# The second layer's output matrix by seven products of blocks per pair instead of eight, with the four pairs written as one order of steps

## Chip, cores and metric

The kernel runs on one core of a Trainium2 chip. The metric is the device time in microseconds (us) of one execution, median of several. TensorE (PE in the rows) does the matrix products, with PEld its weight loads; VectorE (DVE), ScalarE (ACT) and GpSimd (POOL) do elementwise work; SyncE (SP) issues nearly all transfers, which then run on 16 DMA engines.

## The reference

```python
p_packed = sm_attn(p, k, v)                    # 8 x 8 heads, 576 tokens, 32 packed, head size 64
x = heads_joined(sm_attn(q, p_packed, p_packed))            # 4608 x 512
h = x @ w_in                                                # first layer, 512 x 2048
x = (h * sigmoid(1.702 * h)) @ w_out                        # 2048 x 512
g = x @ w_gate                                              # second layer, 512 x 1536
out = (g * sigmoid(g) * (x @ w_val)) @ w_out2               # 1536 x 512, out is 4608 x 512
```

All of it is fp32. The kernel keeps that precision by splitting each operand into a rounded high part and the rest, and by three passes per product (high by high, high by rest, rest by high; `mm3`). A product of 128 x 128 weights with 512 columns is thus three matmuls.

## The kernel before

**The first layer** runs over 8 batches of 576 tokens, two halves each, 16 steps per half. Next to it the next batch's attention and, late, the second layer's weights are made ready: `prep` splits sums and differences of blocks of w_gate and w_val and stores them to `w2s` in DRAM, `split_wo2` splits w_out2 (12 tiles of 128 x 512, kept in SBUF).

**The second layer** takes the 4608 tokens in nine blocks of 512. Block 0 goes alone (`single`, 12 units). The others go in four pairs. For each of 12 column groups m of 128, `quad` computes gate and value of both blocks by seven block products in place of eight; one product is 6 matmuls (`prod`). VectorE and ScalarE add them up in `c1`, `c2`, `c3`, apply tanh, and leave the gated result g of one block in `gh` (split at once by ACT and POOL) and that of the other in the tile `g{m}`. Between the products stands the output matrix of an earlier group: `fill` calls `p5`, which for each of four groups of 128 tokens takes `gh` as weights and w_out2's tile m as 512 columns: 12 matmuls per block and group, into four PSUM banks `acc`. After the 12th group `halve` copies the banks to SBUF, and rows of 512 floats (2 KB) go to `out`, 16 stores of 32 rows per block.

The gv products rotate over four PSUM banks (`ps_h`, `ps_a`, two each). Weights of the next groups come from `w2s` by `load_w` into ten buffers of pool `z_p`. In this part the order on each engine is that in which the tile framework schedules the code; in the first part of the kernel it is a text (`FIRST`) that `issue` reads, with `pin["on"]` set so that each engine keeps that order.

Of the kernel before, what the change touches and what calls it, by code (L numbers as in the profile page):

```python
# [111 lines left out]


@with_exitstack
def kernel(
# [102 lines left out]
    w2s = dram.tile([NM2, 4, P, 2, 512], F32, name="w2s")  # L218

# [529 lines left out]

    def open_m2():  # L750
        p = pools2["m"] = tc.alloc_tile_pool(name="m2", bufs=1, reuse_waits="tile")
# [4 lines left out]
        k2["gh"] = [wo_p.tile([P, 2, TB], F32R, tag="wo1", name="gh") for _ in range(4)]  # L756

# [138 lines left out]
    def gh_of(key):  # L896
        if key not in gt:
            gt[key] = k2["gh"][k2.setdefault("ngh", 0) % 4]
            k2["ngh"] += 1
        return gt[key]  # L900

    def p5(n, m, ts, outs):
        y = gt[n, m]
        if m == 0 and 0 in ts:
            for t in range(4):
                acc[t] = ps_acc.tile([P, 512], F32, tag=f"acc{t}", name="acc")
        for t in ts:
            mm3(acc[t], lambda a: y[:, a, t * P:(t + 1) * P], lambda c: wo2[m][:, c], m == 0, m == NM2 - 1)
            if m == NM2 - 1:
                o = k2[outs[t]]  # L910
                halve(o, acc[t], t % 2)
                b0 = (n * TB + t * P) // 32
                for k0 in range(4):
                    b, j = divmod(b0 + k0, NBLK)
                    eng = ACT if n == NB2 - 1 and k0 % 2 else SP
                    eng.dma_start(out=out[b * S:(b + 1) * S].rearrange("(i n) e -> n i e", n=NBLK)[j],
                                  in_=o[32 * k0:32 * k0 + 32])
        if 3 in ts:
            gt.pop((n, m))

    def split_g2(n, m):
        if n and n % 2 == 0:
            split(gh_of((n, m)), k2["g", m], DVE)

    OUT1, OUT2 = ("c1", "c2", "c3", "s2"), tuple(("g", m) for m in range(4, 8))
    units2 = [(p, m) for p in range(-1, NPAIR) for m in range(NM2)]
    groups = [(n, m) for n in range(NB2) for m in range(NM2)]

    def fill(k, ts=(0, 1, 2, 3)):
        if k >= 0:  # L930
            n, m = groups[k]
            if 0 in ts and k + 2 < len(groups):
                split_g2(*groups[k + 2])
            p5(n, m, ts, OUT1 if n % 2 else OUT2)

    def quad(i, k):

        p, m = units2[i]
        c1, c2, c3, s1, s2, ta, tb = (k2[x] for x in ("c1", "c2", "c3", "s1", "s2", "ta", "tb"))

        def p7(j, a, b):
            q, t = ((ps_h, "h"), (ps_a, "a"))[(i + j) % 2]
            ps = q.tile([P, 512], F32, tag=t, name="gv")
            prod(ps, i, a, b, True)
            return ps

# [24 lines left out]

    def single(m, k):
# [10 lines left out]
        split(gh_of((0, m)), s1, POOL)  # L983
# [32 lines left out]
    for n in range(NU, len(units)):  # L1016
# [35 lines left out]
    for i, (p, m) in enumerate(units2):  # L1052

        k = i - 2 + NM2 * max(p, 0) if p or m > 1 else -1
        last = m == NM2 - 1
        if p < 0:
            single(m, k)
            for part in range(4):
                if m:
                    prep(m + 1, part)  # L1060
            if last:
                load_w(i + 1)
                fill(k + 1)
            for _ in range(2):
                if steps and (len(steps) > 4 or last):
                    steps.pop(0)()
# [53 lines left out]
```

## Time and profile before

| | |
|---|---|
| median of 3 runs | 1642.13 us (1642.01 to 1644.1) |
| profiled execution | 1641.24 us, its span 1639.5 us |
| PE busy | 1618.8 us, 99% of the span |
| PEld / DVE / ACT / POOL busy | 1446.4 / 1138.6 / 764.8 / 279.1 us |
| granted TensorE clock | 0.999 on the mean |
| second layer | from 816 us on: block 0 to 915 us, the pairs to the end |

The span runs from the first to the last instruction; 1.74 us of the execution lie around it. Busy time of an engine is a sum over stages; what a stage costs is read in that stage's own stretch.

### The profile page before, as it was taken

How to read it: one execution, taken by the hardware profiler on the slowest of the kernel's cores; microseconds unless marked ns; L12 is line 12 of the kernel's file. 1: busy time of each engine (PE TensorE's matmuls, PEld its weight loads, DVE VectorE, ACT ScalarE, POOL GpSimd, SP SyncE). 2: the span in 40 equal slices, each digit the busy share in tenths (PEclk: the TensorE clock that was granted, in tenths of full speed). 3: DMA queues.
4: the chain of work that ended last, by engine and by line, in shares of the span. 5: the costliest groups of instructions: out<-in, count | busy, mean ns of one | idle time of the engine just before them, and what ended most of it. 6: DMA issues, size and time to landing. Idle time of an engine off the chain costs nothing.

```text
span 1639.5 us, 25914 instructions
## 1 busy us (share of the span) xinstructions
PE 1618.8 (99%) x9346; PEld 1446.4 (88%) x9346; DVE 1138.6 (69%) x2152; ACT 764.8 (47%) x1629; POOL 279.1 (17%) x235
## 2 busy tenths in 40 slices
PE   8999999999999999999999999999999999999998
PEld 7799999999999999999988888888888888888887
DVE  7988786876869777685894566756566656846562
ACT  5876667565656757564652222332233222422222
POOL 1342131231313123020221110000100001000010
PEclk9999999999999999999999999999999999999999
DMA  9987757475655737253887444435443544425411
GB/s 316 315 268 225 208 170 241 156 223 149 214 186 167 243 114 241 73 194 104 288 315 279 155 154 159 149 109 163 156 158 110 174 139 155 143 79 185 141 46 52
DMA packets 169345, 291.66 MB, mean 178 GB/s; under 512 B 58624, under 2 KB 96000, under 8 KB 169216
## 3 DMA queue, kind: packets, MB, share of 16 engines
q1 hardware_dynamic: 168832, 289.47, 54.1%
q8 instruction: 74, 1.21, 0.3%
q10 hardware_dynamic: 384, 0.52, 0.1%
q14 instruction: 55, 0.45, 0.1%
HBM read 227.02 MB, written 62.91 MB: 177 GB/s over the span
## 4 chain that ended last, share of the span: by engine, by line
PE 83%; DVE 8%; issue 4%; ACT 2%; DMA 2%; POOL 0%; SPq 0%; DVEq 0%; ACTq 0%
PE acc L151 35%; PE gv L151 30%; PE h L151 10%; PE sc L151 3%; PE zp L151 2%; PE pv L151 2%; DVE z L151 1%; DVE gh L151 1%; DVE g L151 1%; DVE x L151 1%; PE idle L151 1%; DMA wh<-win 1%; ACT z L151 1%; PE a1T L151 0%; DVE c L151 0%
## 5 line engine op out<-in xcount | busy, mean ns | idle before, releaser
L151 PE MATMUL gv<-xh,w 128*128 128x512 f32 x2304 | 554.4, 389 | 0.0
L151 PEld LDWEIGHTS gv<-xh,w 128*128 128x128 f32 x2304 | 432.5, 188 | 89.7
L151 PE MATMUL acc<-gh,wo 128*128 128x288 f32 x3072 | 454.0, 296 | 0.8 <-DVE gh L151 0.6
L151 PEld LDWEIGHTS acc<-gh,wo 128*128 128x128 f32 x3072 | 424.3, 188 | 5.7 <-DVE gh L151 1.4
L151 PE MATMUL acc<-wo,gh 128*128 128x512 f32 x1296 | 326.9, 389 | 0.4
L151 PEld LDWEIGHTS acc<-wo,gh 128*128 128x128 f32 x1296 | 243.0, 188 | 52.0 <-DVE c L151 1.7
L151 PE MATMUL h<-a,z 128*128 128x288 f32 x1536 | 251.3, 298 | 1.0 <-DVE g L151 0.9
L151 DVE TENSOR_TENSOR gh<-g,gh 128x288 fp32r<-128x288 f32 (+1 forms) x285 | 170.5, 598 | 89.4 <-ACT gh L151 86.7
L151 PEld LDWEIGHTS h<-a,z 128*128 128x128 f32 x1536 | 220.5, 188 | 9.9 <-DVE g L151 3.0
L151 ACT CAST gh<-g 128x288 fp32r<-128x288 f32 (+1 forms) x304 | 140.4, 462 | 157.1 <-DVE g L151 104.4
L151 POOL TENSOR_TENSOR gh<-s,gh 128x512 fp32r<-128x512 f32 x60 | 82.3, 1372 | 699.1 <-ACT gh L151 655.4
L151 DVE TENSOR_TENSOR c<-gv,c 128x512 f32<-128x512 f32 x192 | 132.3, 689 | 84.0 <-ACT tb L151 56.6
L151 ACT CAST gh<-s 128x512 fp32r<-128x512 f32 x60 | 37.3, 621 | 248.0 <-DVE s L151 248.0
L151 DVE SCALAR_TENSOR_TENSOR g<-sig,h 128x288 f32<-128x288 f32 x256 | 114.1, 446 | 42.8 <-ACT sig L151 39.8
L151 ACT ACTIVATE sig<-h 128x288 f32<-128x288 f32 x256 | 104.5, 409 | 78.2 <-PE h L151 75.9
L151 DVE TENSOR_TENSOR ta<-gv,c 128x512 f32<-128x512 f32 x96 | 66.1, 689 | 83.3 <-PE gv L151 83.3
L151 POOL TENSOR_TENSOR z<-z,z 128x512 fp32r<-128x512 f32 x51 | 69.7, 1367 | 151.6 <-ACT z L151 151.6
L151 DVE TENSOR_TENSOR z<-zp,z 64x512 f32<-64x512 f32 (+1 forms) x120 | 81.9, 682 | 14.9 <-ACT z L151 12.2
L151 ACT ACTIVATE s<-c 128x512 f32<-128x512 f32 x48 | 30.4, 632 | 96.5 <-DVE c L151 96.5
L151 PE MATMUL zp<-wh,E 128*128 128x512 f32 x224 | 66.9, 400 | 5.0 <-DVE z L151 2.5
L151 ACT COPY z<-zp 64x512 f32<-64x512 f32 x112 | 65.1, 581 | 12.4 <-PE zp L151 9.7
L151 ACT ACTIVATE s<-ta 128x512 f32<-128x512 f32 x48 | 30.3, 632 | 69.0 <-DVE ta L151 69.0
(133 smaller groups left out, 1504.0 us busy)
## 6 DMA issues: line engine op xcount, KB each, us to landing
w<-w2s SPq DMA_DIRECT2D x144, 512.0 KB, 3.2
wh<-win SPq DMA_DIRECT2D x96, 512.0 KB, 4.0
w2s<-w SPq DMA_DIRECT2D x36, 512.0 KB, 3.7
w<-w2s SPq DMA_DIRECT2D x48, 256.0 KB, 2.7
vt<-in_v_dram SPq DMA_DIRECT2D x80, 128.0 KB, 3.4
x2d<-x SPq DMA_DIRECT2D x16, 576.0 KB, 3.2
w2d<-f SPq DMA_DIRECT2D x36, 256.0 KB, 3.1
w64in<-in_moe_w_in_dram SPq DMA_DIRECT2D x16, 512.0 KB, 8.7
```

Source lines behind the costliest of these rows:

```text
L151: x = getattr(self.engine, name)(*a, **k)
```

## The change

**Seven products for the output matrix.** For a pair of blocks, g (1024 tokens by 1536) and w_out2 (1536 by 512) are seen as 2 x 2 blocks each. Seven products of block sums replace eight products of blocks. Each has 6 chunks of 128 along the inner dimension (numbered k) and two halves e of 128 output columns; one `pt n e` is three matmuls of 512 columns. There are 42 chunks n per pair, listed in `SUMS`: n 0 to 11 belong to products 0 and 1 in turn, then six each to products 2 to 6. Weights and columns change sides: a 128 x 128 piece of the weight sums is now loaded as weights and the 512 tokens of g are the columns, so that the result comes out transposed.

**Weight sums.** `sums` computes the four sums of blocks of w_out2 during the last batch of the first layer (steps 6 to 17), splits them on ACT and POOL and stores them to a new DRAM tensor `w5s`; `split_wo2` stores its own tiles there too (18 stores of 256 KB). `load_wo2` starts at step 18 instead of 5. In the pairs, `lw5` loads two chunks (512 KB) at a time into four buffers.

**Sums of g.** `ts` (four per k, DVE) turns the gated results, now in `g1` and `g`, into block sums in place; `hi n` (ACT) and `lo n` (POOL or DVE) split chunk n into one of five `gh` buffers. `fd` and `f4` add the banks' contents into the output blocks, `tr` transposes 32 x 32 squares on DVE, and `od j e a` stores 32 output columns of 512 tokens: pieces of 32 floats (128 bytes), in two transfers where the 512 tokens cross a batch.

**One written order.** The text `SECOND` lists 2452 steps for the four pairs (675, 625, 625, 527; a plus sign marks a step of the next pair), read by `issue` with `pin` on. Besides those above: `pr j x` is product x of unit j (6 matmuls), `c1`, `t1`, `tb`, `t2` are the unit's ACT steps, `e1` to `e6`, `b5`, `u1`, `u2`, `g1`, `g2` its DVE steps, `xa`, `xh`, `xl` prepare the next pair's tokens, `lw` and `lx` load gate weights and tokens.

```diff
+    TURN = [NK * (j % 2) + j // 2 for j in range(NM2)]
+    SUMS = [(j % 2, j // 2) for j in range(NM2)] + [(j, k) for j in range(2, 7) for k in range(NK)]
...
         split(wo2[m], x32.pop(("o", m)), POOL if m % 2 else DVE)
         load_wo2(m + 5)
+        h, k = divmod(m, NK)
+        SP.dma_start(out=w5_of(h, k), in_=wo2[m][:, :, :256].bitcast(F32))
+        if h:
+            SP.dma_start(out=w5_of(5, k), in_=wo2[m][:, :, 256:].bitcast(F32))
...
+        def pt(n, e):
+            j, k = SUMS[n]
+            b = 2 * (j % 2) + e
+            if k == 0:
+                ab[b] = ps_acc.tile([P, 512], F32, tag=f"acc{b}", name="acc")
+            w, y = w5[p, n // 2][:, n % 2], oper[p, n]
+            mm3(ab[b], lambda a: w[:, a, e * P:(e + 1) * P], lambda c: y[:, c], k == 0, k == NK - 1)
...
+        def fd(j, e):
+            ps, v, u = ab[2 * (j % 2) + e], (c1, c2)[e], (c3, s2)[e]
+            if j == 0:
+                ACT.activation(v, ps, AF.Copy, scale=0.5)
...
+                    eng = ACT if p == NPAIR - 1 and j == 6 and a % 2 else SP
+                    eng.dma_start(out=out[b * S:(b + 1) * S].rearrange("(i n) e -> i n e", n=NBLK)[:, k:k + c, e0:e0 + 32],
+                                  in_=y[:, t:t + c])
...
             if u == 5:
+                load_sums(0)
+            if 6 <= u < 18:
+                sums(*divmod(u - 6, 2))
+            if u == 18:
                 for i in range(5):
                     load_wo2(i)
```

Two pieces of the text for the second pair, the end of its last unit and the passage to the next pair:

```
pr 11 6; hi 11; xa 0 0; lw5 8; hi 14; b5 11; lx 5; xh 0 4; lo 14 dve; lo 11 pool; pt 10 0; +lw 2 1; xh 0 6; e6 11;
pt 10 1; fd 0 0; e5 11; pt 11 0; t2 11; xa 0 1; hi 15; pt 11 1; u2 11; xh 0 2; pt 12 0; lw5 9; lo 15 pool; fd 0 1;
hi 16; pt 12 1; g2 11; pt 13 0; ts 5 1; pt 13 1; lo 16 dve; hi 17; pt 14 0; lw5 10; fd 1 0; hi 18; lo 17 pool
```

**Where instructions now stand.** On TensorE, in the middle of a pair, one unit before (gv are the gate and value products, acc the output matrix, w and wo their tiles):

```order
L151 MATMUL gv<-xh,w_12558 128x512 x12
L151 MATMUL acc<-wo_10914,gh 128x512 x3
L151 MATMUL gv<-xh,w_12560 128x512 x6
L151 MATMUL gv<-xh,w_12562 128x512 x6
L151 MATMUL acc<-wo_10914,gh 128x512 x3
L151 MATMUL gv<-xh,w_12564 128x512 x6
L151 MATMUL acc<-wo_10914,gh 128x512 x3
L151 MATMUL gv<-xh,w_12560 128x512 x6
L151 MATMUL acc<-wo_10914,gh 128x512 x3
L151 MATMUL gv<-xh,w_12562 128x512 x6
```

and the last unit of the first pair with what follows it in the changed kernel (here w under acc is a tile of weight sums):

```order
L338 MATMUL gv<-xh,w_12843 128x512 x12
L338 MATMUL gv<-xh,w_12862 128x512 x6
L338 MATMUL gv<-xh,w_12883 128x512 x6
L338 MATMUL acc<-gh,w_12101 128x512 x3
L338 MATMUL gv<-xh,w_12917 128x512 x6
L338 MATMUL gv<-xh,w_12862 128x512 x6
L338 MATMUL acc<-gh,w_12101 128x512 x3
L338 MATMUL gv<-xh,w_12883 128x512 x6
L338 MATMUL acc<-gh,w_12102 128x512 x12
L338 MATMUL acc<-gh,w_12103 128x512 x12
L338 MATMUL acc<-gh,w_12104 128x512 x12
L338 MATMUL acc<-gh,w_12101 128x512 x12
```

A unit holds two acc groups instead of four, and after the last unit 32 chunks (n 10 to 41) follow each other with no gv product between them.

On ScalarE at that place, before (a unit and the copies of finished banks to g):

```order
L151 COPY tb<-gv 128x512
L151 ACTIVATE s_10093<-c_11142 128x512
L151 COPY c_11141<-gv 128x512
L151 ACTIVATE g_11133<-acc 128x512
L151 ACTIVATE s_10092<-ta 128x512
L151 ACTIVATE g_11135<-acc 128x512
L151 CAST gh<-s_10092 128x512
```

and now, the second pair from `hi 11` to `hi 16` (c1 and c2 from acc are `fd 0 0` and `fd 0 1`, s2 from c2 is `t2 11`, xh the next pair's tokens):

```order
L338 CAST gh_11278<-g1_12096 128x512
L338 CAST gh_11276<-g1_12098 128x512
L338 CAST xh_10084<-ta_10095 128x512
L338 CAST xh_10082<-x32_13663 128x512
L338 ACTIVATE c1_11272<-acc_13713 128x512
L338 ACTIVATE s2_10094<-c2_11273 128x512
L338 CAST gh_11277<-g1_12098 128x512
L338 CAST xh_10086<-s1_10093 128x512
L338 ACTIVATE c2_11273<-acc_13739 128x512
L338 CAST gh_11278<-g1_12099 128x512
```

The copy that empties the bank of `pt 12 1` stands behind three other steps, two of which wait for VectorE.

On SyncE at a block's output, before (four stores of 32 rows of 512 floats for each bank):

```order
L151 DMA x_14426<-x2d 128x512
L151 DMA out_dram<-c_11141 32x512 x4
L151 DMA out_dram<-c_11142 32x512 x4
L151 DMA out_dram<-c_11143 32x512 x4
L151 DMA out_dram<-s_10093 32x512 x4
L151 DMA x_14428<-x2d 128x512
```

and now, in the first units of a following pair:

```order
L338 DMA out_dram<-g_12098 32x14x32
L338 DMA w_13555<-w2s 128x512
L338 DMA out_dram<-g_12099 32x4x32
L338 DMA out_dram<-g_12099 32x12x32
L338 DMA w_13568<-w2s 128x1024
L338 DMA out_dram<-g_12099 32x4x32
L338 DMA out_dram<-g_12099 32x12x32
```

Stores of pieces of 32 floats stand between the loads of the next units' weights, two transfers for each `od`.

## Rows read from the trace of the kernel before

**Rows 1.** The page: busy time by engine, and the chain's shares.

```profile
PE 1618.8 (99%) x9346; PEld 1446.4 (88%) x9346; DVE 1138.6 (69%) x2152; ACT 764.8 (47%) x1629; POOL 279.1 (17%) x235
...
PE 83%; DVE 8%; issue 4%; ACT 2%; DMA 2%; POOL 0%; SPq 0%; DVEq 0%; ACTq 0%
```

**Rows 2.** Stretches: length, busy us (instructions) by engine, clock, DMA share, GB/s.

```profile
1089.25:1269.20 179.95, 179.81 (x793) 148.56 (x793) 111.57 (x170) 53.20 (x90) 15.54 (x12) 1.00 0.45 147
1269.20:1449.20 180.00, 179.86 (x794) 148.65 (x793) 111.56 (x170) 53.21 (x90) 15.54 (x12) 1.00 0.42 139
```

**Rows 3.** Chain that ended last, in order of time: start, length, matmuls.

```profile
914.74 21.76 PE gv L151 x96
...
1242.38 26.83 PE acc L151 x117
...
1596.06 36.05 PE acc L151 x159
```

**Rows 4.** Groups of instructions by form: busy us, mean ns of one.

```profile
L151 PE MATMUL acc<-wo,gh 128*128 128x512 f32 x1296 | 326.9, 389 | 0.4
...
L151 DVE TENSOR_TENSOR c<-gv,c 128x512 f32<-128x512 f32 x192 | 132.3, 689 | 84.0 <-ACT tb L151 56.6 <-PE gv L151 22.2 <-DVE c L151 0.9
...
L151 POOL TENSOR_TENSOR gh<-s,gh 128x512 fp32r<-128x512 f32 x60 | 82.3, 1372 | 699.1 <-ACT gh L151 655.4 <-issue 43.8
...
L151 DVE STREAM_TRANSPOSE T<-raw 128x576 f32<-128x576 f32 x52 | 39.7, 768 | 9.7 <-POOL Th L151 7.3 <-DMA w<-in_moe_w_gate_dram 1.1 <-DMA w2d<-f 1.1
...
L151 ACT CAST gh<-s 128x512 fp32r<-128x512 f32 x60 | 37.3, 621 | 248.0 <-DVE s L151 248.0
```

**Rows 5.** Order of time: POOL's subtraction beside VectorE's work.

```profile
816.47 0.41 DVE L151 TENSOR_TENSOR ws<-w,w 128x256 f32<-128x256 f32 x1
...
838.56 1.35 POOL L151 TENSOR_TENSOR gh<-s,gh 128x512 fp32r<-128x512 f32 x1 [4.23 <-ACT gh L151]
838.68 1.51 DVE L151 TENSOR_TENSOR ws<-w,w 128x256 f32<-128x256 f32 x1
...
1279.62 1.29 POOL L151 TENSOR_TENSOR gh<-s,gh 128x512 fp32r<-128x512 f32 x1 [44.02 <-ACT gh L151]
...
1280.07 0.69 DVE L151 TENSOR_TENSOR c<-gv,c 128x512 f32<-128x512 f32 x1 [1.24 <-ACT tb L151]
```

**Rows 6.** Stretches with five vt loads (393.1 us on), then block 8's first stores.

```profile
394.00:395.00 1.00, 1.00 (x9) 1.00 (x9) 0.92 (x4) 0.25 (x1) 0.00 (x0) 1.00 0.66 150
395.00:396.00 1.00, 1.00 (x10) 1.00 (x9) 0.91 (x4) 0.40 (x2) 0.00 (x0) 1.00 0.96 217
396.00:397.00 1.00, 1.00 (x10) 1.00 (x9) 1.00 (x4) 0.92 (x4) 0.74 (x1) 1.00 1.06 239
397.00:398.00 1.00, 1.00 (x10) 1.00 (x9) 1.00 (x4) 0.58 (x3) 0.19 (x1) 1.00 0.23 50
...
1601.00:1602.00 1.00, 1.00 (x6) 0.83 (x5) 0.46 (x1) 0.99 (x2) 0.00 (x0) 1.00 0.59 146
```

**Rows 7.** Stretches around the passage to the second layer.

```profile
750.00:760.00 10.00, 10.00 (x78) 10.00 (x77) 3.73 (x9) 3.74 (x9) 0.00 (x0) 1.00 0.26 91
...
790.00:800.00 10.00, 10.00 (x78) 10.00 (x77) 9.49 (x18) 6.88 (x16) 2.45 (x3) 1.00 0.97 344
...
810.00:820.00 10.00, 9.32 (x56) 8.18 (x55) 8.38 (x17) 5.44 (x13) 1.69 (x1) 1.00 0.92 307
...
880.00:890.00 10.00, 10.00 (x46) 8.29 (x45) 2.06 (x3) 1.29 (x3) 1.28 (x1) 1.00 0.89 314
```

**Rows 8.** SyncE in order of time: start, issuing time, transfers.

```profile
393.10 2.59 SPq L151 DMA_DIRECT2D vt<-in_v_dram  x5
...
913.36 7.39 SPq L151 DMA_DIRECT2D out_dram<-g  x16
920.85 6.48 SPq L151 DMA_DIRECT2D w<-w2s  x5
```

**Rows 9.** DMA issues by line: count, KB each, median us to landing.

```profile
w<-w2s SPq DMA_DIRECT2D x144, 512.0 KB, 3.2
...
vt<-in_v_dram SPq DMA_DIRECT2D x80, 128.0 KB, 3.4
```

**Rows 10.** Order of time: the end of the execution.

```profile
1632.14 0.60 ACT L151 ACTIVATE g<-acc 128x512 f32<-128x512 f32 x1 [8.44 <-PE acc L151]
...
1634.90 1.86 ACTq L151 DMA_DIRECT2D out_dram<-g  x4
```

More of the change, by code (lines that the diff above doesn't have):

```diff
@@ L827, in split_wo2, with load_sums, sums @@
         load_wo2(m + 5)
+        h, k = divmod(m, NK)
+        SP.dma_start(out=w5_of(h, k), in_=wo2[m][:, :, :256].bitcast(F32))
+        if h:
+            SP.dma_start(out=w5_of(5, k), in_=wo2[m][:, :, 256:].bitcast(F32))
+    def load_sums(k):
+        if k < NK:
+            for h in range(2):
+                x32["s", k, h] = raw_tile()
+                SP.dma_start(out=x32["s", k, h], in_=w2d[3 * (k + NK * h) + 2])
+    def sums(k, late):
+        s = k2["ws"]
+        if not late:
+            load_sums(k + 1)
+            a, b = (x32.pop(("s", k, h)).rearrange("p (h x) -> p h x", h=2) for h in range(2))
+            for o, x, y, op in ((1, a[:, 1], b[:, 1], ALU.add), (0, s[:, 1], a[:, 0], ALU.subtract),
+                                (2, a[:, 0], a[:, 1], ALU.subtract), (3, b[:, 0], s[:, 0], ALU.subtract)):
+                DVE.tensor_tensor(out=s[:, o], in0=x, in1=y, op=op)
+            return
+        for o, x in enumerate(("ta", "tb", "s1", "s2")):
+            y = k2[x].rearrange("p (a x) -> p a x", a=2).bitcast(F32R)
+            split(y, s[:, o], POOL)
+            SP.dma_start(out=w5_of((2, 4, 3, 6)[o], k), in_=y.bitcast(F32))
     XS = [(c, x) for c in range(2) for x in ("11", "12", "22", "21")]
@@ L905, in p5 @@
             for t in range(4):
                 acc[t] = ps_acc.tile([P, 512], F32, tag=f"acc{t}", name="acc")
-        for t in ts:
+        for t in range(4):
             mm3(acc[t], lambda a: y[:, a, t * P:(t + 1) * P], lambda c: wo2[m][:, c], m == 0, m == NM2 - 1)
             if m == NM2 - 1:
-                o = k2[outs[t]]
+                o = k2["g", 4 + t]
                 halve(o, acc[t], t % 2)
-                b0 = (n * TB + t * P) // 32
                 for k0 in range(4):
[L914 to L934, printed above, removed]
@@ L1051 @@
         load_x2(0, i)
[L1052 to L1066, printed above, removed]
-            if last:
-                fill(k + 2)
-                while steps:
-                    steps.pop(0)()
-            continue
-        load_w(i + 1)
-        quad(i, k)
-        if m == NM2 - 2:
-            for j in range(5):
-                load_x2(p + 1, j)
-        if last:
-            steps = x_steps(p + 1)
-            for j in range(NM2):
-                fill(k + 1 + j)
-                for _ in range(2):
-                    if steps:
-                        steps.pop(0)()
-            while steps:
-                steps.pop(0)()
-    for k in range(len(groups) - 2, len(groups)):
-        fill(k)
+    for m in range(NM2):
+        single(m, m - 2)
+        for part in range(4):
+            if m:
+                prep(m + 1, part)
+        if m == NM2 - 1:
+            load_w(NM2)
+            fill(m - 1)
+        for _ in range(2):
+            if steps and (len(steps) > 4 or m == NM2 - 1):
+                steps.pop(0)()
+    fill(NM2 - 1)
+    while steps:
+        steps.pop(0)()
+    open_g()
+    pin["on"] = True
+    for p, text in enumerate(SECOND):
+        issue(text, pair(p), pair(p + 1))
     pools2["m"].release()
```

358 lines of the change are left out of this document (314 added, 44 removed).

## Prediction

> **What bounds the kernel now.** I read the page first: PE is busy for 99% of the span and holds 83% of the chain [rows 1], so the question for every edit is whether it takes matmuls out of PE's queue or makes PE wait. The stretches say so for the part that changes: in a pair of the second layer (180 us) PE stands idle for 0.14 us, VectorE works 111.6 us, ScalarE 53, POOL 15.5, and the transfers take 45% of the DMA engines [rows 2]. The clock is granted in full there. The chain in order of time gives the price of one matmul of 512 columns when nothing interrupts: 36.05 us for 159 is 0.2267 us, and the gv products cost the same, 21.76 us for 96 [rows 3]. (The 389 ns that the groups show for one is its latency [rows 4]; matmuls overlap.) A pair's 504 gv and 288 acc matmuls make 792 x 0.2267 = 179.5 us, its whole length.
>
> **What is removed.** Per pair 7 x 6 x 2 x 3 = 252 acc matmuls stand for 288. The shape is the same (128 x 128 weights, 512 columns), so I price them alike: 36 x 0.2267 = 8.16 us per pair, 32.64 us for four. Block 0 and the first layer keep their matmuls. Nothing else in the change shortens anything, so 32.6 us is the most it can give.
>
> **What is added, and where it could make PE wait.**
>
> *A unit's chain: nothing.* A unit with one chunk beside it lasts 42 matmuls and 6, 10.9 us. VectorE has 11 steps in it and two `ts` on average, 13 x 0.69 [rows 4] = 9.0 us, and waits once for tanh (0.62, as ScalarE's other steps). That is 9.6 of 10.9, and the four gv banks let it be three products (4 us) late. I count nothing; if POOL holds it up on top (below), 1.4 us more per unit would make 11.0, and 10 units in 4 pairs would lose 0.1 each, 4 us.
>
> *The bank of `pt 12 1`: 4.5 us.* Chunk 12 reuses the banks of product 0, which `fd 0 0` and `fd 0 1` must have emptied. From the end of `pt 10 0` PE reaches `pt 12 1` after four groups of 0.68 us, 2.7 us. In that time ScalarE has, in its order, `fd 0 0`, `t2 11`, `hi 15`, `xh 0 2` and `fd 0 1`: five times 0.62 [rows 4] = 3.1 us, so PE waits 0.4 at the least. `t2` also waits for `e6 11` and `xh 0 2` for `xa 0 1`, and on VectorE these come behind `lo 14 dve`, which POOL's `lo 11` can hold up. Walking both queues from `e3 11` on with 0.62, 0.69 and 1.37 us, I find that `e6` starts 1.7 us after its product, `xa 0 1` is done 1.9 us after that, and `fd 0 1` 1.5 us after PE wants the bank. I take 1.5 (bounds 0.4 and 3, when POOL comes between once more) in three pairs. The last pair has no `xh` there, and I count none.
>
> *POOL and VectorE in the long run of chunks: 1.5 us.* The rows show that some of VectorE's work stops while POOL subtracts: a subtraction of 256 columns with both inputs in SBUF takes 0.41 us alone and 1.51 beside POOL's of 1.35 us, while an addition with a PSUM input took its usual 0.69 beside one [rows 5]. From `pt 12 0` to `pt 36 0` PE needs 24 x 1.36 = 32.6 us. POOL has 13 `lo` (17.8 us), VectorE 29 steps with two SBUF inputs (20.0 us) and 13 others (9 us), which can run beside POOL. If the first two exclude each other, they need 37.8 us, 5.2 more than PE. Five `gh` buffers let `hi n` start when `pt n-5` is done, 5.4 us ahead of `pt n`; less the split (0.62 and 1.37) that leaves a lead of 3.5 us, and the means of 0.69 and 1.37 themselves hold some such waits. I take 0.5 us a pair for the first three (bounds 0 and 6, as under the rivals). In the last pair, which prepares no tokens, the sums are 16 and 11 steps, 26 us, and fit.
>
> *Small stores: nothing, but this is the weakest item.* 32 `od` per pair store 512 pieces of 128 bytes each. The nearest rows are the vt loads, 512 pieces of 256 bytes: five of them took 0.66 + 0.96 + 1.06 + 0.23 = 2.91 us of all engines [rows 6], 0.58 each. A 64 KB store in rows of 2 KB, one per 0.46 us [rows 8], used 0.59 of them, 0.28 [rows 6]. I take 0.58, the end with as many pieces. From `pt 19` to the next pair's `pr 1 4` PE works 47.6 us; in it fall the 32 stores (18.6 us) and 12 `lw5`, five `lw` and two `lx`, 9.2 MB, at 344 GB/s [rows 7] 26.7 us. The sum of 45.3 fits, with little left. SyncE issues 62 to 64 transfers for `od` at 0.46 to 0.52 us [rows 8] and 19 others, about 40 of the 47.6 us. `lw5` stands six chunks (8.2 us) ahead of its use and lands in 3.2 [rows 9], so 5 us of lateness are free.
> No row of this trace stores pieces under 512 bytes. The Trainium skill speaks against such stores: "DMA: Bandwidth & Descriptors", Specifications, says that under 512 bytes the DMA engine reads, modifies and writes. If that means twice the 0.58 us, an estimate from its rule, the sum would be 64 us for 47.6 and the forecast that of the last rival; the sum here does not use it.
>
> *The passage from the first layer: 1 us.* `sums` adds 24 additions of 0.41 us [rows 5], 24 ACT and 24 POOL splits and 6 MB of stores at steps 6 to 17, where VectorE works 3.7 of 10 us and the DMA engines 0.26 [rows 7]. `split_wo2` adds 18 stores of 256 KB, 4.7 MB, where the engines are already at 0.92 to 0.97 [rows 7]: 13.7 us at 344 GB/s, with some 5 us free in 40. Transfers run up to 9 us late. Behind them wait the weights of `single`, which `prep` has ready about 25 us before use at the end (VectorE is down to 2.1 of 10 us from 880 us on [rows 7], while block 0 lasts to 915) but only a few us at the start. I take 1 (0 to 9).
>
> *First weights of pair 0: 0.3 us.* `lw 1 0` now stands behind the 16 stores of block 0 on SyncE, which end at 920.8 [rows 8]; it lands 3.2 later [rows 9], at 924.0. PE, with the pair begun at 914.74 [rows 3], wants it after 9.5 us, at 924.3. Bounds 0 and 2.
>
> *The end: 0.5 us.* Now PE's last nine matmuls follow the chain's end at 1632.1 [rows 3] to 1634.1, the last issue ends at 1636.8 [rows 10], the span at 1639.5: 5.4 us, 2.7 of it after that issue. Then `fd` 0.69, `tr` 0.68 (512 of 576 columns of 0.77 [rows 4]), two stores on each of two queues 1.0, and 2.7: 5.1; with SyncE's queue of earlier stores up to 1 more. I take 5.9.
>
> **The sum**, against the profiled execution of 1641.24: 1641.24 - 32.64 + 4.5 + 1.5 + 1.0 + 0.3 + 0.5 = 1616.4. The median of the runs stands 0.9 above that execution, so I forecast 1617.3, 1.5% faster.
>
> **Rivals.**
> *All waits hidden* (0.13): ScalarE and VectorE run a little faster than walked, 1641.24 - 32.64 + 0.9 = 1609.5. For it: the present pairs have no wait of PE at all.
> *POOL and VectorE* (0.13): half of the 13 others cannot hide, so the long run needs 37.8 + 4.5 = 42.3 us, 9.7 over, 6.2 after the lead, in three pairs 18.6 instead of 1.5: 1634. For it: the 1.51 us row. Against: POOL's share in the rows is small, and the forms with one PSUM input don't suffer.
> *The passage jams* (0.07): 8 us more there, 1625. For it: a DMA share of 0.97; against: VectorE is idle at 880.
> *Small stores* (0.09), the one on the other side: if a store of 512 pieces takes twice what the vt load of as many takes, 1.16 us, the stretch of 47.6 us needs 64, 16 late, 11 after the free 5, in each of three pairs; in the last, 32 stores and nine `lw5` need 37 + 14 us within the 34 from `pt 17` to the end, 17 late. 1617.3 + 33 + 17 = 1667. The gain left, 24 us, is gone when each pair loses 6, that is at 26.7 + 32c = 47.6 + 5 + 6, c = 1.0 us per store. For it: no row shows such a store, and transfers out of SBUF may cost more than those into it. Against: 256-byte pieces cost 18 ns each on an engine (2.91 us x 16 engines / 2560 pieces). The page's rule, named above, would bring this case about.
>
> **Numbers.** The forecast (1611 to 1624) has 0.58. The range goes from the case in which all is hidden, 1609, to 1630, part of the way to the POOL case; the small stores and the rest of that case stay out, under 2 in 10. 0.2% (3.3 us) is about what a measurement of this kernel can tell from no change. Faster by more: 0.58 + 0.13 + 0.13 + 0.07 = 0.91. Of the small stores' 0.09, 0.03 for a price near 1.0 us (no change) and 0.06 for a higher one.
>
> **What would show it.** Right: acc matmuls 1152, 144 of them block 0's; pairs of about 172 to 174 us with PE idle 1 to 3 us in each, in one wait on acc for ScalarE about 14 us after the last unit begins; VectorE over 85% busy; DMA near 65%. The POOL case shows as `gh` subtractions on VectorE of 1 us and more on the mean and PE waiting for gh between chunks 20 and 36. The small stores show as PE waiting for `w5` loads, or VectorE for stores from `c3`, with a DMA share near 1. What would make me wrong beyond the rivals is a price of the new matmuls other than 0.2267 us.

## The result, and the profile after

The changed kernel takes 1625.68 us (median of 4 runs, 1624.27 to 1629.31) where the kernel before takes 1642.88 beside it: a ratio of 0.9898, with a 95% interval of 0.988 to 0.9916. That is 1.0% faster, inside the forecast range of 1609 to 1630 and 8.4 us above the forecast of 1617.3. The profiled execution took 1625.42 us, its span 1623.7, 15.8 us less than the span of before.

The page of the changed kernel, busy time by engine and the chain's shares, answers to [rows 1]; below it stand the two stretches that answer to [rows 2], and PE's groups by form (answering to the first of [rows 4]).

```profile
PE 1591.4 (98%) x9202; PEld 1421.3 (88%) x9202; DVE 1312.8 (81%) x2356; ACT 803.9 (50%) x1717; POOL 396.4 (24%) x319
...
PE 81%; DVE 8%; issue 4%; DMA 3%; ACT 2%; SPq 1%; POOL 1%; ACTq 0%; POOLq 0%; DVEq 0%
```

```profile
1086.00:1260.00 174.00, 171.38 (x752) 140.93 (x753) 152.67 (x216) 60.72 (x106) 38.94 (x27) 1.00 0.70 215
1260.00:1434.00 174.00, 172.17 (x759) 141.82 (x758) 152.14 (x216) 61.23 (x107) 40.01 (x27) 1.00 0.71 215
```

```profile
L338 PE MATMUL acc<-gh,w 128*128 128x512 f32 x972 | 236.7, 390 | 6.1 <-ACT c L338 3.8 <-DVE gh L338 2.0 <-DMA w<-w5s 0.3
L338 PE MATMUL acc<-wo,gh 128*128 128x512 f32 x144 | 34.3, 389 | 0.0
```

PE has 144 matmuls fewer and is still the chain. In a pair VectorE now works 152 of 174 us (0.88), and the transfers take 0.70 of the DMA engines. With the 36 matmuls of 512 columns that read xh in the last pair, the acc matmuls are 972 + 144 + 36 = 1152, as forecast. But PE, which waited 0.14 us in a pair before, now waits.

Where the 15.8 us come from is read from the beginnings of PE's stretches in order of time. The first row is the first product of `single` before; the others are, in the changed kernel, the first product of `single`, the first products of pairs 1, 2 and 3, and the last stretch of matmuls.

```profile
816.65 2.66 PE L151 MATMUL gv<-xh,w 128*128 128x512 f32 x11
```

```profile
821.19 2.00 PE L338 MATMUL gv<-xh,w 128*128 128x512 f32 x8
...
1094.80 5.38 PE L338 MATMUL gv<-xh,w 128*128 128x512 f32 x23
...
1268.98 6.28 PE L338 MATMUL gv<-xh,w 128*128 128x512 f32 x27
...
1442.76 7.42 PE L338 MATMUL gv<-xh,w 128*128 128x512 f32 x32
...
1606.35 8.32 PE L338 MATMUL acc<-xh,w 128*128 128x512 f32 x36
```

`single` begins at 821.19 where it began at 816.65, so the passage lost 4.5 us. Pairs 1 and 2 take 174.2 and 173.8 us, and the last, in which PE waits for nothing, 171.9 from 1442.76 to 1614.67, where 180.0 stood before. From there to the span's end at 1623.7 it takes 9.0 us, not 5.4. Between 821.19 and 1614.67 there are 793.5 us, 24.0 less than before. So the sum is +4.5 - 24.0 + 3.6 = -15.9.

PE's waits in the four pairs are these (waited for: us in total, times, longest).

```profile
PE acc L338 <- ACT c L338: 3.8, 3, 1.3
PE acc L338 <- DVE gh L338: 2.0, 3, 0.9
PE gv L338 <- DMA w<-w2s: 0.8, 1, 0.8
PE acc L338 <- DMA w<-w5s: 0.3, 1, 0.3
```

They are 6.9 of the 8.6 us that 24.0 lacks of 32.6. The other 1.7 stand in no row of waits. They belong to the same eight waits: at the wait of 1.26 us of pair 1 the matmuls before and behind it start 1.65 us apart and the next one 0.34 later, where 0.23 is usual in that pair, so that a wait costs 0.2 to 0.3 us more than its row says.

The first wait is that of `pt 12 1` for `fd 0 1`, at the forecast place. In order of time, pair 0:

```profile
1047.53 1.75 POOL L338 TENSOR_TENSOR gh<-g,gh 128x512 fp32r<-128x512 f32 x1 [7.79 <-ACT gh L338]
...
1048.04 1.79 DVE L338 TENSOR_TENSOR gh<-g,gh 128x512 fp32r<-128x512 f32 x1
...
1050.46 0.64 ACT L338 ACTIVATE s<-c 128x512 f32<-128x512 f32 x1 [0.84 <-DVE c L338]
...
1051.66 0.62 ACT L338 CAST xh<-s 128x512 fp32r<-128x512 f32 x1
...
1052.26 0.60 ACT L338 ACTIVATE c<-acc 128x512 f32<-128x512 f32 x1
...
1052.91 3.26 PE L338 MATMUL acc<-gh,w 128*128 128x512 f32 x13 [1.26 <-ACT c L338]
```

VectorE's `lo 14` lasts 1.79 us beside POOL's `lo 11`, `e6 11` follows it, ScalarE waits 0.84 for that with `t2 11`, and `hi 15` and `xh 0 2` go ahead of `fd 0 1`, whose end at 1052.86 releases PE.

The wait for gh comes from another place than I had thought. The rows follow the token load `lx 6` of pair 0 to PE.

```profile
1072.99 0.42 SPq L338 DMA_DIRECT2D x<-x2d  x1
...
1077.18 0.62 ACT L338 CAST xh<-x 128x512 fp32r<-128x512 f32 x1 [2.46 <-DMA x<-x2d]
...
1080.23 0.62 ACT L338 CAST xh<-x 128x512 fp32r<-128x512 f32 x1 [1.39 <-DMA x<-x2d]
...
1086.16 5.52 PE L338 MATMUL acc<-gh,w 128*128 128x512 f32 x23 [0.48 <-DVE gh L338]
```

ScalarE stands 2.46 and 1.39 us at `xh 1 6` and `xh 1 1`, with the gh casts of the next chunks behind them, and PE meets the late gh.

The passage lost its time at the end of a half-batch. The rows show POOL's last splits of `sums`, VectorE's first additions for the next weights, PE, and the copies `x<-acc` that free its banks.

```profile
779.88 1.60 POOL L338 TENSOR_TENSOR s<-ws,s 128x256 fp32r<-128x256 f32 x2
...
779.95 1.82 DVE L338 TENSOR_TENSOR ws<-w 128x256 f32<-128x256 f32 x2 [0.45 <-POOL tb L338]
...
780.94 0.66 PE L338 MATMUL acc<-gh,wo 128*128 128x288 f32 x3 [0.31 <-ACT x L338]
...
783.28 0.45 DVE L338 TENSOR_SCALAR x<-acc 128x288 f32<-128x288 f32 x1
...
783.79 2.53 PE L338 MATMUL acc<-gh,wo 128*128 128x288 f32 x9 [2.19 <-DVE x L338]
```

The two additions take 1.82 us beside POOL's splits, where two alone take 0.82 [rows 5]; four of them and the work between stand ahead of the copy, which comes 2.8 us after ScalarE's first copy of the same sums (780.49). Behind the wait the granted clock fell. The stretch from 780 to 792 us has a mean of 0.72:

```profile
780.00:792.00 12.00, 9.50 (x49) 9.03 (x48) 9.57 (x21) 5.88 (x14) 2.37 (x3) 0.72 0.89 282
```

### The profile page after: what moved, and what is told of

Its sections match the earlier page's. It is cut to its first block, busy times and chain, and to the rows that moved or that the text cites. A ratio compares the mean times of both kernels' runs of the same rounds, so it can differ in the third digit from the quotient of the medians.

```text
span 1623.7 us, 26484 instructions
## 1 busy us (share of the span) xinstructions
PE 1591.4 (98%) x9202; PEld 1421.3 (88%) x9202; DVE 1312.8 (81%) x2356; ACT 803.9 (50%) x1717; POOL 396.4 (24%) x319
## 4 chain that ended last, share of the span: by engine, by line
PE 81%; DVE 8%; issue 4%; DMA 3%; ACT 2%; SPq 1%; POOL 1%; ACTq 0%; POOLq 0%; DVEq 0%
PE acc L338 32%; PE gv L338 30%; PE h L338 10%; PE sc L338 3%; PE zp L338 3%; PE pv L338 2%; DVE z L338 1%; DMA x<-x2d 1%; DVE g L338 1%; DVE gh L338 1%; PE idle L338 1%; SPq L338 1%; DVE c L338 1%; ACT z L338 1%; DVE x L338 1%
## 5 line engine op out<-in xcount | busy, mean ns | idle before, releaser
L338 PE MATMUL gv<-xh,w 128*128 128x512 f32 x2304 | 537.8, 389 | 0.8 <-DMA w<-w2s 0.8
L338 POOL TENSOR_TENSOR gh<-g,gh 128x512 fp32r<-128x512 f32 (+1 forms) x124 | 171.2, 1384 | 556.6 <-ACT gh L338 485.6
L338 ACT CAST gh<-g 128x288 fp32r<-128x288 f32 (+1 forms) x418 | 208.1, 505 | 163.7 <-DVE g L338 118.2
L338 PE MATMUL acc<-gh,w 128*128 128x512 f32 x972 | 236.7, 390 | 6.1 <-ACT c L338 3.8
L338 DVE TENSOR_TENSOR gh<-g,gh 128x288 fp32r<-128x288 f32 (+1 forms) x294 | 192.8, 656 | 54.0 <-ACT gh L338 50.8
L338 PEld LDWEIGHTS acc<-gh,w 128*128 128x128 f32 x972 | 181.5, 188 | 47.6 <-ACT c L338 5.2
L338 DVE TENSOR_TENSOR c<-gv,c 128x512 f32<-128x512 f32 x192 | 131.7, 688 | 20.2 <-ACT tb L338 11.9
L338 ACT COPY tb<-gv 128x512 f32<-128x512 f32 x48 | 28.2, 587 | 202.7 <-PE gv L338 202.7
L338 ACT COPY c<-gv 128x512 f32<-128x512 f32 x48 | 28.2, 587 | 107.4 <-PE gv L338 92.5
L338 DVE TENSOR_TENSOR g<-g,g 128x512 f32<-128x512 f32 x96 | 68.2, 741 | 0.1
```

Of the source, the lines that this page charges most:

```text
L338: x = getattr(self.engine, name)(*a, **k)
```

## The experiments

Each kernel was run beside the kernel before. The ratio of the changed kernel is 0.9898, and each ratio below is to the same base. What an edit does in its place is read from the stretches of one trace each. Six traces share the order of the first three pairs (the changed kernel twice, and e3 to e6); in them the first pair takes 174.9 to 178.5 us, pair 1 173.8 to 174.7 and pair 2 173.0 to 174.2, so that less than about 1 us in one pair shows nothing.

**The bank (e1_bank).** Unit 11's gate is taken out of the way of `fd 0 1`.

```
+        def cv(j):
+            return k2["t2", NK - 1] if j == NM2 - 1 else c2      # in e2, e3, b5, e6, t2, u2
-  fd 0 0; e5 11; pt 11 0; t2 11; xa 0 1; hi 15; ... lo 15 pool; fd 0 1;
+  fd 0 0; e5 11; pt 11 0; fd 0 1; t2 11; xa 0 1; hi 15; ... lo 15 pool;
```

> One edit to the changed kernel: unit 11 keeps its value sum in the tile t2 5, which is free at that time, in place of c2, and in pairs 0 to 2 the copy fd 0 1 stands on ScalarE ahead of t2 11, hi 15 and xh 0 2. Theory (the bank of chunk 12 is held because fd 0 1 writes c2 and so stands behind unit 11's gate): the wait of acc for ScalarE (1.26 us in each of three pairs, 1.5 with the gap behind it) goes, and nothing takes its place: pairs of 172.7 us where they took 174.2, 1621.3 us, 4.5 less. Rival (VectorE, 0.87 busy in a pair, is the limit there, and the wait only shows it): the time comes back as waits of acc for gh before chunk 36, and the time stays within 1 us of 1625.7.

1630.47 us, ratio 0.9921 (0.9906 to 0.9935). The theory is false. The bank's wait is gone, but pairs 1 and 2 take 174.9 and 174.5 us, 0.7 more each than in the changed kernel's trace (no gain, though hardly more than the spread), and PE waits in the pairs for these:

```profile
PE acc L338 <- DMA w<-w5s: 3.5, 5, 1.2
PE acc L338 <- DVE gh L338: 3.5, 4, 1.1
PE acc L338 <- DVE s L338: 1.7, 3, 1.0
PE gv L338 <- DVE c L338: 1.4, 1, 1.4
```

**The token loads (e2_tokens).**

```
-  lo 29 pool; lx 6; pt 26 0; hi 30; lw5 16; lx 7; pt 26 1;
+  xa 0 3; lx 6; lx 7; od 1 1 0; pt 23 0;
```

> One edit to the changed kernel: the token loads lx 6 and lx 7 are issued three and a half chunks earlier (behind xa 0 3, at chunk 22, not at 26). Theory (the waits for gh at the end of the run of chunks, 1.4, 1.2 and 0.8 us of PE in pairs 0 to 2, come from these loads: they land 4.2 to 5.3 us after their issue, xh 1 6 stands two chunks behind them on ScalarE and waits 2.5 us, xh 1 1 waits 1.4, and the gh casts stand behind both): ScalarE's waits for x2d shrink to under 0.5 us, PE's waits for gh go, 2 to 3.5 us less, 1622.2 to 1623.7. Rival (the term of the prediction: POOL's subtractions stop VectorE's in the long run of chunks): the waits for gh stay at 2.0 us together, the time within 1 us of 1625.7.

1624.35 us, ratio 0.9886 (0.9864 to 0.9907). The median is only 1.3 us lower and the intervals overlap; what is shown is in the trace. ScalarE no longer waits for x2d, pairs 1 and 2 take 172.9 and 173.0 us, and PE ends at 1612.36, 2.3 us earlier than in the changed kernel. Its waits in the pairs hold none for gh:

```profile
PE acc L338 <- ACT c L338: 3.8, 3, 1.3
PE gv L338 <- DVE c L338: 1.4, 1, 1.4
PE acc L338 <- DMA w<-w5s: 0.5, 1, 0.5
```

(In the changed kernel the rows give 0.5, 0.9 and 0.6 us for pairs 0 to 2, less than the expectation has.) The six traces named above, with the late loads, show 2.0 to 2.6 us of it; of the five kernels with the early loads (this one, e7_both, c1_three, c2_all, f_nopool) none shows any.

**The sums earlier (e3_sums).**

```
-            if u == 5:
+            if u == 3:
                 load_sums(0)
-            if 6 <= u < 18:
+            if 4 <= u < 16:
```

> One edit to the changed kernel: the 12 steps of sums and their first load run two units earlier (units 4 to 15, not 6 to 17). Theory (the passage lost its time where the first half-batch ends: the combination of the next weights shares the tile ws with sums, so VectorE waits for POOL's last split with the two halving copies behind it, PE stands 2.5 us for them, and the granted clock falls to 0.50 for the 4 us after): both waits and the fall of the clock go, the first product of the first block of the second layer starts at 816.5 to 818, not 821.35, 3.5 to 5 us less, 1621 to 1622.2. Rival (the term of the prediction: 4.7 MB more of stores on DMA engines at 0.92 to 0.97 make the weights late): the product still starts at 821, the time within 1 us of 1625.7.

1626.89 us, ratio 0.9896 (0.9882 to 0.9911): inconclusive, since the edit moved nothing. The last splits of `sums` ran at 780.7 and not at 779.9: in this stage the scheduler, not the text, sets the order, and the first loads were issued at 744 in both. PE's wait of 2.5 us stayed.

**The copies first (e5_order)** asks the same with the order itself fixed.

```
+            on, pin["on"] = pin["on"], pin["on"] or (b, t) == (B - 1, 0)
             for e in range(NE):
                 halve(x[:, e], acc[e][:, :HS], e % 2)
+            pin["on"] = on
...
+                pin["on"] = m == 0
                 combine(m)
+                pin["on"] = False
```

> One edit to the changed kernel: VectorE's order at the end of the first half-batch is fixed, so that the four additions that combine the next weights (on the tile ws, which sums uses too) come behind the two halving copies and not ahead of them. sums itself stays where it is. Theory (the passage lost its time there: the additions stand still beside POOL's last splits, the copies of the finished sums behind them, PE idle for 2.5 us and then at a granted clock of 0.50): the copies run at 780.5 to 781.5, PE's waits of 0.3 and 2.2 us go and the clock stays at 1.00, the first product of the second layer starts at 816.5 to 818 where it started at 821.2; 3.5 to 5 us less than the changed kernel's 1625.7. Rival (the additional stores, as the prediction had it): the product still starts at 821, whatever VectorE does before.

1623.37 us, ratio 0.9881 (0.9867 to 0.9896). In the trace `single` begins at 815.95, 5.2 us earlier, with all the stores in place. The median fell by 2.3 us only, less than the theory has it: the traced execution, 1621.11 us, is the fastest of four. VectorE's copy and PE in order of time, then the stretch of the clock:

```profile
780.37 2.40 PE L338 MATMUL acc<-gh,wo 128*128 128x288 f32 x12 [0.32 <-ACT x L338]
780.65 0.45 DVE L338 TENSOR_SCALAR x<-acc 128x288 f32<-128x288 f32 x1
```

```profile
780.00:792.00 12.00, 11.56 (x85) 11.16 (x85) 9.78 (x23) 8.67 (x21) 3.60 (x4) 1.00 0.94 312
```

PE does 85 matmuls in these 12 us, not 49, at a DMA share of 0.94 where it was 0.89: the full DMA engines were not the cause. The fall of the clock seems to be little of the 4.5 us: in e6_sp (below) PE stood the same 2.5 us, the clock stayed at 1.00, and `single` still began at 820.91; PE, earlier by then, waited 0.8 us in all for VectorE's late g, near 803 and 809 us.

**The last stores (e4_tail, e6_sp).** First four small stores of sum 5 to ScalarE, then all stores to SyncE.

```
-  eng = ACT if p == NPAIR - 1 and j == 6 and a % 2 else SP
+  eng = ACT if p == NPAIR - 1 and (a % 2 if j == 6 else j == 5 and e == 0 and c < 4) else SP   # e4_tail
+  eng = SP                                                                                     # e6_sp
```

> One edit to the changed kernel: in the last pair four of the 8 KB stores of the sum 5 (od 5 0) are issued by ScalarE, not SyncE. Theory (the end is set by SyncE's queue: 23 stores of 0.70 us each from 1605.16 on, while the last transpose is done at 1616.14): SyncE ends 4 x 0.70 = 2.8 us earlier, at 1618.5, and the span with it; ScalarE with eight stores of 1.24 us from 1608.5 on ends at 1618.4; 2.5 us less, 1623.2. Rival (what takes 0.70 us is not the issue itself but the landing of earlier stores, which the next one waits for): the end moves by less than 1 us, or comes later since ScalarE's stores wait in the same way.

1628.62 us, ratio 0.9907 (0.9892 to 0.9922), longer by what the first pair took, which the edit does not touch (2.9 us more), and by 1.3 us in the last pair, 1.0 of it a wait for w5. The end took 8.4 us after PE's (1618.58 to 1627.0), not 9.0. The rival holds: SyncE's 19 stores took 15.0 us, 0.79 each where the 23 had taken 0.70, so 0.70 was no price of an issue. In the program each transfer waits on one of eight semaphores, given out in turn over both queues. Three stores of SyncE and two of ScalarE, as the program has them (the number is the place on the engine):

```
1193 L338 DMA out_0_dram<-g1_12098 32x14x32 [waits DMAHW6_49]
1194 L338 DMA out_0_dram<-g1_12098 32x2x32 [waits DMAHW0_49]
1195 L338 DMA out_0_dram<-g1_12098 32x14x32 [waits DMAHW2_49,DVE_49]
...
1626 L338 DMA out_0_dram<-g1_12099 32x16x32 [waits DMAHW0_49,DVE_49]
1627 L338 DMA out_0_dram<-g1_12099 32x16x32 [waits DMAHW2_49]
```

1194 and 1195 wait for the landing of ScalarE's 1626 and 1627, which are issued only when sum 6 is there, at 1612.1. SyncE's rows of the changed kernel, in three stretches of time, show two gaps, from 1611.2 to 1613.9 and from 1616.8 to 1617.9:

```profile
1605.16 6.02 SPq L338 DMA_DIRECT2D out_dram<-g  x10
...
1613.92 2.91 SPq L338 DMA_DIRECT2D out_dram<-g  x6
...
1617.93 3.40 SPq L338 DMA_DIRECT2D out_dram<-g  x7
```

> One edit to the changed kernel: in the last pair SyncE issues all stores, the four of ScalarE too. Theory (an issue costs 0.32 to 0.5 us, but each transfer waits until the one eight places ahead of it has landed, counted over both queues in one order; ScalarE's early places, issued only at 1612.1 and 1616.2, hold SyncE's stores behind them for 2.7 and 1.1 us): without them SyncE issues without these gaps, ends at about 1618.2, and from PE's end to the span's end it takes 5.8 to 6.5 us, not 9.0: 2.5 to 3.2 us less. Rival (the 23 stores of SyncE are the bound by their number; 27 of them on one queue take longer): the end comes 9 us or more after PE's, the time the same or up to 2 us longer.

1624.45 us, ratio 0.989 (0.9876 to 0.9905); the end took 7.7 us (1615.05 to 1622.8). The gaps are gone, as the theory has it, but the 27 stores in a row last until 1620.4, not 1618.2, and the end lies between what theory and rival say:

```profile
1605.46 14.95 SPq L338 DMA_DIRECT2D out_dram<-g  x27
```

So the end had two causes, 0.55 us for each issue and the order in which the two queues share the semaphores.

**Bank and tokens (e7_both).**

> Two edits to the changed kernel: that of the bank (fd 0 1 early, its tile free) and that of the token loads (lx 6 and lx 7 at chunk 22). The first alone made the pairs 0.7 us longer, the second alone 1.0 shorter. Theory (with the bank's wait gone PE only reaches the late gh and w5 1.5 us sooner; with the loads early there is nothing left for it to wait for): the pairs take 171.6 to 172 us where the second alone has 172.9, 1620 us. Rival (VectorE's folds wait for the stores of the sums, s2 above all, and set the pace of the chunks): waits of acc for s and for w5 stay at 1 us and more in a pair, pairs of 172.5 to 173.5 us, 1622 to 1625.

1627.11 us, ratio 0.9906 (0.9892 to 0.9921). The rival holds, and the loss is greater than it said: pairs 1 and 2 take 173.7 and 173.8 us, 0.8 more than with the tokens alone, and PE waits 2.1 us for s, 2.6 for w5 and 1.1 for xh in the pairs.

**Long rows (e8_rows).**

```
-  out=out[b * S:(b + 1) * S].rearrange("(i n) e -> i n e", n=NBLK)[:, k:k + c, e0:e0 + 32], in_=y[:, t:t + c]
+  out=out[r:r + 32, 32 * t:32 * (t + c)], in_=where(j, e)[1][32 * a:32 * a + 32, 32 * t:32 * (t + c)]   # r: 32 rows for each store
```

> The changed kernel with the od stores' bytes put in long rows: as many transfers from the same tiles at the same places, but each writes 32 rows of 1792 and 256 bytes (or of 2 KB), not 512 pieces of 128 bytes; the rows of three sums out of four, and with them the output, lie elsewhere. Theory (the pieces cost time only on the DMA engines, which have room; the waits are those of the order): pairs 1 and 2 within 0.5 us of 174.2 and 173.8, the end within 1 us of 9.0, the time within 2 us of 1625.7; the DMA share of a pair falls from 0.70 to about 0.55. Rival (the pieces make the w5 loads, the first weights and the landings late): the waits for w5 and w2s go, the end shortens to 6 to 7 us, 3 to 5 us less in all.

1622.94 us, ratio 0.9876 (0.9859 to 0.9892). Each theory is half right. Pairs 1 and 2 take 173.0 and 173.0 us, 1.2 and 0.8 less, with no wait for gh (ScalarE waits 2.2, 1.1 and 2.0 us for x2d in pairs 0 to 2, where it waited 3.9, 3.1 and 2.8), and the end takes 6.6 us. PE's waits for w2s and w5 stay, 1.2 and 0.6 us. From `single` to the span's end the trace is 4.5 us shorter; the median is only 2.7 lower, and in the trace `single` began at 824.89, 3.7 us later, where the edit touches nothing. At the end SyncE waits 2.3 us for landings, not 4.0, with the semaphores given out in another order, so the end does not give the price of the pieces by itself. The DMA share (the number before the last) falls only from 0.70 and 0.71 to these:

```profile
1086.00:1260.00 174.00, 172.14 (x757) 141.59 (x756) 153.82 (x217) 61.32 (x106) 39.33 (x28) 1.00 0.66 214
1260.00:1434.00 174.00, 172.74 (x762) 142.56 (x762) 152.89 (x216) 61.45 (x107) 40.60 (x28) 1.00 0.67 216
```

0.04 of 174 us over 32 stores is 0.2 us per store more than in long rows. The price itself stands at the end of the changed kernel, where from 1611 to 1624 us nothing but these stores is moved (queue, packets, MB, share of 16 engines):

```profile
q1 hardware_dynamic: 5014, 0.61, 28.0%
q10 hardware_dynamic: 2112, 0.26, 11.9%
```

0.399 of 13 us for 0.87 MB is 0.39 us of all engines for 64 KB. The same count in this run, from 1611 us on, gives 0.27 for the long rows (33.5% of 11.9 us for 0.98 MB). I had taken 0.58.

**The changed kernel again, three edits, and all (again, c1_three, c2_all)**, run side by side. The third edit puts the last stores in this order, and c2_all adds the bank and gives sum 1 other tiles.

```
-  od 5 1 0; pt 38 1; od 6 0 1; od 5 1 1; pt 39 1; od 6 0 3; ... od 5 1 3; fd 6 1; od 6 0 0; od 6 0 2; tr 6 1; od 6 1 0; ...
+  od 5 1 0; pt 38 1; od 5 1 1; ... od 5 1 3; od 6 0 0; od 6 0 1; od 6 0 2; od 6 0 3; fd 6 1; tr 6 1; od 6 1 0; ...
+  eng = ACT if p == NPAIR - 1 and j == 6 and (e == 0 or a % 2) else SP     # ordered behind the stores ahead of it
+  where(1, e): k2["t2", 4 + e] for (c3, s2)[e]                             # c2_all only
```

> The changed kernel once more, without an edit, beside the two kernels that follow: 1624 to 1627 us. In six traces of kernels that share its first pair, the wait for the first weights of pair 0 took 0.24 to 1.7 us and those for w5 at the end of that pair 0.3 to 1.3, so I expect the same pairs 1 to 3 within 0.3 us (174.2, 173.8, 171.9) and a first pair that differs by up to 2 us.

1625.78 us (1624.19 to 1628.01), ratio 0.9894 (0.9881 to 0.9908); pairs 1 to 3 173.8, 173.7 and 172.4 us, up to 0.5 off the expected ones, and 2.0 us of wait for the first weights in a first pair 2.3 us longer.

> Three edits to the changed kernel: the token loads at chunk 22, VectorE's order at the end of the first half-batch, and a new order of the last stores (all of sum 5 on SyncE ahead of the first of sum 6; of sum 6 six on ScalarE, two on SyncE). Theory (each loss has its own cause, so they add): the second layer starts 5 us earlier, pairs 1 and 2 take 172.9, and the span ends 5.5 to 6.5 us after PE, not 9.0: 5.2 + 2.3 + 3 = 10.5 less, 1614 to 1617 us. Rival (the transfers are one resource, and what is gained at one place is paid at the next, as in the run of the bank and the tokens together): 1618 to 1621.

1616.03 us (1615.02 to 1619.95), ratio 0.9839 (0.9825 to 0.9852): it beats both kernels, and the interval lies clear of that of the changed kernel run beside it. The theory holds in the time, which is 9.8 us less than that of the changed kernel beside it. `single` begins at 817.35, pairs 1 and 2 take 172.9 and 173.1, and the end 6.1 us.

```profile
817.35 16.53 PE L337 MATMUL gv<-xh,w 128*128 128x512 f32 x72
```

Against the changed kernel's first trace the gains are 3.8 us in the passage (not 5.2), 2.3 in the pairs and 3.0 at the end, 9.1 together. A little of the rival is in it too: the last pair took 173.0 us, 1.0 more, 0.7 of it a wait for w5.

> As the kernel of three edits, and fd 0 1 early with its own tile for unit 11, and the transposed sum 1 written to t2 4 and t2 5 in place of c3 and s2, so that the folds of product 3 do not wait for the stores of sum 1. Theory (those stores were what took the place of the bank's wait): no wait of acc for s, pairs of 171.6 to 172.2, 2.5 to 4 us less than the kernel of three edits. Rival (VectorE itself, over 0.87 busy in a pair, or w5 behind the stores on SyncE): waits for w5 or gh of about 1 us stay, pairs of 172.7 to 173.5, the time that of the kernel of three edits within 1.5 us.

1615.84 us (1614.17 to 1619.09), ratio 0.9835 (0.9822 to 0.9849). In this kernel `ts 5 3` still reads t2 5 after sum 1 is put there, so a part of the last products is computed from other numbers; the order of the work is as described. No wait for s is left, but the rival holds: pairs 1 and 2 take 173.7 and 173.3 us, and the time is that of the three edits. PE's waits in the pairs:

```profile
PE acc L337 <- DMA w<-w5s: 3.2, 5, 1.2
PE acc L337 <- ACT xh L337: 1.3, 2, 0.9
PE gv L337 <- DMA w<-w2s: 0.5, 1, 0.5
```

**POOL's help taken away (f_nopool).** From c1_three, `lo n pool` became `lo n dve` for all n from 13.

> The kernel of three edits (1616.0 us), and the 15 subtractions lo of each pair's long run of chunks that POOL does (13, 15, 17 to 41 odd; 17 and 36 to 41 in other places in the last pair) done by VectorE. Theory (beside each of POOL's subtractions of 1.3 us one of VectorE's with two SBUF inputs stands still; in 40 us of the run 11 of its 61 instructions last 8.5 us longer than 0.69, which is what 13 to 15 subtractions of its own, 0.61 apart, would take, 8 to 9 us): VectorE's instructions in the run last 0.69 throughout, its sum stays within 1 us of 41.7 in 40, the pairs stay within 1 us of 172.9, the time within 3 us of 1616. Rival (POOL's work is help that costs VectorE little): VectorE lacks 8 us in 40, waits for gh of 4 to 8 us appear in each of the first three pairs, 1628 to 1640 us.

1619.56 us (1617.73 to 1620.16), ratio 0.9858 (0.9842 to 0.9875). The rival is refuted. Forty us of pair 1's run of chunks with POOL's help (c1_three), and VectorE's subtractions in them by form:

```profile
1222.00:1262.00 40.00, 39.77 (x175) 32.96 (x176) 39.00 (x49) 20.08 (x35) 18.89 (x14) 1.00 0.73 211
```

```profile
L337 DVE TENSOR_TENSOR gh<-g,gh 128x512 fp32r<-128x512 f32 x13 | 12.1, 934 | 0.1
```

And the same without it (f_nopool):

```profile
1222.00:1262.00 40.00, 38.53 (x170) 31.25 (x169) 36.48 (x61) 21.74 (x37) 0.00 (x0) 1.00 0.70 210
```

```profile
L337 DVE TENSOR_TENSOR gh<-g,gh 128x512 fp32r<-128x512 f32 x26 | 17.8, 684 | 0.2
```

VectorE does 12 instructions more and is busy 2.5 us less. (These rows count 49 and 61 instructions of VectorE; the 61 of the expectation, for the kernel with POOL's help, are not what its row shows. The 41.7 there are the lengths added up; records of instructions that follow at once overlap by 0.08 us, and so added up the lengths are about 41.2 us in either kernel.) The run of chunks stands 2.7 us later in f_nopool; shifted by as much, the stretch gives VectorE the same 36.48. The time is 3.5 us longer, a little over the 3 that I allowed, but the intervals overlap, and 1.1 us of it in the traces is a later `single`. Pairs 1 and 2 take 173.8 and 174.1 us. PE waits for no gh; for the bank it waits 1.47 us in place of 1.27, and for the first weights and w5 0.6 us more. The rest stays open.

## Why the forecast was right, and where 8 us stayed

**The matmuls: right.** 36 fewer at 0.2267 us should make 8.2 us a pair, and the pair without waits is 8.1 shorter. A unit's chain cost nothing, as forecast: inside the units PE waits for nothing but the first weights.

**The bank of `pt 12 1`: place and size right, its meaning not.** 1.26 us in each of three pairs, forecast 1.5, none in the last. But I priced it as a loss that its removal would give back. It was not one: with it gone (e1_bank, e7_both, c2_all) PE meets late w5, xh, s or gh within the same pair. VectorE is 39 of 40 us busy there in c1_three and 60.8 of 63 in c2_all, so I take it that VectorE and the transfers that follow its results set the pace; no run separates the two (c2_all with POOL's subtractions taken away would).

**POOL and VectorE in the long run: the step that failed in its cause, not in its size.** I put 1.5 us there and PE waited 2.3 (gh and w5). Yet the waits for gh came from two token loads that I costed at nothing: used two chunks after their issue, landing 4.2 us and more later. Two moved words removed them (e2_tokens). That the size came out near was luck. The exclusion itself is real (VectorE's subtractions take 934 ns on the mean with POOL's help and 684 without), but with early loads PE waits for no gh with it or without it (c1_three, f_nopool). The Trainium skill, "SBUF — State Buffer", Who interferes with whom, says that an instruction of VectorE with two SBUF inputs contends with one of GpSimd that reads SBUF, under an exclusive lock; the trace agrees (`lo 14` took 1.79 us beside POOL's 1.75).

**Small stores: nothing, about right.** 0.39 us of all engines per store, not 0.58, and far from the break-even of 1.0. What they did cost is about 1 us a pair in one trace (e8_rows), near the spread; that it goes through the token loads is inferred, since with long rows the wait for gh is gone too.
The rule of the Trainium skill named in the forecast ("DMA: Bandwidth & Descriptors", Specifications: under 512 bytes read, modify, write) would, taken as twice the price, have made 1.16; the trace, with 0.39, does not bear that price out. Whether the engines read and modify, no run shows.

**The passage: mis-sized, 4.5 for 1.0, by a wrong mechanism.** I wrote that VectorE "works 3.7 of 10 us" at steps 6 to 17 and so hid `sums`, and looked for the loss in the DMA share. The mean hid the order: VectorE's additions, slowed beside POOL's splits, stood ahead of two copies for which PE waits (e5_order).

**First weights: 0.8 for 0.3**, and 0.2 to 2.0 over the executions, within the bounds of 0 to 2.

**The end: mis-sized, 9.0 for 5.9.** I counted two stores on each of two queues behind the last transpose, and allowed 1 us for SyncE's earlier stores. SyncE still had 23 to issue at 1605.16, eight of them behind that transpose, and stood 3.8 us for semaphores that ScalarE's stores held.

Together: 3.5 us more than forecast in the passage, 2.3 in the pairs (8.6 for 6.3, the first weights in it) and 3.1 at the end are 8.9; the median lies 0.3 above the profiled execution where I had added 0.9, which leaves 8.3 of the 8.4. The rival of the jammed passage named 1625, nearly the time measured, but its jam did not come; nor did the other rivals. That the time lies within the range is owed to the matmul term and to a range of 21 us: four of the terms beside it (POOL, the passage, the first weights, the end) had a wrong mechanism or less than half of the size.

## What to carry to other kernels

A wait that PE shows is only the first of the things that are late: before you price its removal, ask how busy the engine behind it is in that stretch, and what arrives next. Work that is "hidden" on an engine with idle time still has a place in its order, and a mean busy share says nothing about who stands behind it. Count the transfers at the end of a kernel one by one, with the semaphores they take in turn over all queues.

## What was not expected of the hardware

POOL's subtractions free no time on VectorE: 13 of them in 40 us save VectorE 12 instructions and lengthen the others by more (39.00 us busy with, 36.48 without). Pairs 1 and 2 were still 0.8 and 1.0 us shorter with them, for a reason that stays open.

After PE had stood idle for about 2.5 us among matmuls of 288 columns, the granted clock fell: from 784 to 788 us it was 0.50 in the changed kernel, the lower level of 1.2 GHz, and it was back at 1.00 from 792 on. Of the nine traces with that wait, eight show a fall there (0.50 to 0.78 in the lower of the stretches 784 to 788 and 788 to 792) and one, e6_sp, none; the four without the wait show none. What decides in the ninth stays open.
